# Reordering three early loads, one warm-up matmul less, and splitting a matmul chunk around the gathered rows' transposes

## The chip, the cores and the metric

The kernel runs on one core of a Trainium2 chip. The metric is the device time of one execution in microseconds (us); lower is better. The engines of the core are TensorE (PE, with its weight loads shown apart as PEld), VectorE (DVE), ScalarE (ACT), GpSimd (POOL) and SyncE (SP). Loads and stores are issued by SP, ACT or POOL and carried by the core's DMA engines.

## The reference

x is 2048 tokens of 640 features in bf16. It is normalized per token, and two branches on the normalized tokens xn are added to x:

```python
xn = _layernorm(x, axis=-1)
# branch A: linear attention, 32 heads of 20, phi(t) = where(t > 0, t + 1, exp(t)) + 1e-6
q, k, v = split(xn @ wqkv)
kv = einsum("bhsd,bhse->bhde", phi(k), v);  z = sum over s of phi(k)
a = (phi(q) @ kv) / (phi(q) @ z + 1e-6) @ wo
# branch B: one expert on the 8 tokens with the largest r = xn @ w_r
idx = argsort(-r)[:8]
y = (silu(xn[idx] @ w_gate) * (xn[idx] @ w_up)) @ w_down * sigmoid(r[idx])
b = xn + scatter_add(idx, y)
out = x + a + b
```

## The kernel before

The tokens are 16 tiles of 128. The order of the instructions on every engine is written out by hand; each engine and each queue works in the order of the program, and waits are semaphores between them.

*Start.* `ld_x(t0, t1, q)` (L114) loads tiles of x on queue q. SP issues tile 0, the first three fifths of the k weights (`wk[:, 0:3]`, L119), the router row `wrow` (L122), then tiles 2, 3, 4 and 5, the q weights `wq` and tiles 6 and 7. ACT's queue issues tile 1 and the last two fifths of the k weights (`wk[:, 3:5]`, L120). Meanwhile PE runs `N_WARM` matmuls on constants (L231) whose result nobody reads, and later `N_FILL` small ones (L368).

*Per tile.* `stats` (L238 to L241, DVE) makes mean and variance; `small` (L245 DVE, L246 POOL) makes the inverse deviation `rs` by a power on POOL; `center` subtracts the mean and `norm` (L266, DVE) scales by `rs`. `tr_mm` (L273, PE) transposes a tile by five 128x128 transposes into a PSUM bank, and `tr_ev` (L279 on ACT, L281 on DVE) copies it out. `k_mm(t, h)` (L302, PE) multiplies the tile with half h of the k weights in five steps over 128 features each: steps 0 to 2 need the first part of the weights, steps 3 and 4 the second. `k_act` (L313, L314, ACT) makes exp and relu, `k_stt` (L322, DVE) joins them to phi(k) in `pk`, and `g_mm` (L330, L332, PE) adds pk-transposed times xn to the sums over all tiles, which stay in PSUM. The first tiles are written out by hand: PE does the transposes of tile 0, turns the router row into a column of the k weights (L389), runs the two fills, then `k_mm(0, 0)`, the transposes of tile 1, `k_mm(0, 1)`, `k_mm(1, ...)`, the transposes of tile 2 and `g_mm(0, ...)`. DVE does `norm(0)`, `stats(2)`, `small(2)`, the two copies of tile 1's transposes, `center(2)`, `norm(2)`, `k_stt(0)`, `norm(1)` and so on. A loop over tiles 3 to 15 follows, with some chunks of q in it.

*Middle.* The sums leave PSUM (`gt`), the eight tokens are picked (L580 to L594, DVE), and POOL gathers their rows from memory into `xsel` by an indirect DMA (L597). In the meantime PE makes chunks of q: `q_next(bk)` takes the next chunk (128 features by 512 tokens) and calls `q_mm` (L345), five matmuls into PSUM bank bk; `q_fin` and `q_fin_d` turn it into phi(q) in `pqT`. `den_mm` (L675) makes denominators. `moe_xt(3)` transposes the gathered rows (L611) into bank 3, DVE copies them to `xsT` (L612), and `moe_gu_mm` (L628) multiplies them with the gate and up weights; `moe_silu` (L634 to L636, ACT) and the rest of the expert follow, with `kv_mm` (L714), `m_mm` (L733) and the stores `m_dma` (L747, SP) between them.

*End.* `out_mm` (L837) makes the output of the 16 tiles, ACT and DVE add the rest, and the tiles are stored.

Of the kernel before, what the change touches and what calls it, by code (L numbers as in the profile page):

```python
# [8 lines left out]
P = 128  # L9
# [5 lines left out]
KC = D // P  # L15
# [12 lines left out]
BF16 = mybir.dt.bfloat16  # L28
# [3 lines left out]
AF = mybir.ActivationFunctionType  # L32
ALU = mybir.AluOpType

N_WARM = 11
N_FILL = 2
PE_TR = 4
Q_ALL = [(m, b) for b in range(4) for m in range(KC)]
# [2 lines left out]
Q_TAIL = Q_ALL[Q_LOOP:]  # L41
# [7 lines left out]
def kernel(  # L49
# [16 lines left out]
    sp, act, dve, pool, pe = nc.sync, nc.scalar, nc.vector, nc.gpsimd, nc.tensor  # L66
# [9 lines left out]
    def sb(shape, dt, name):  # L76
        return big.tile(shape, dt, tag=name, name=name)
# [3 lines left out]
    def bank(i):  # L81
        return ps[:, i, :]

    def bankb(i):
        return ps[:, i, :].bitcast(BF16)
# [28 lines left out]
    def ld_x(t0, t1, q):  # L114
        q.dma_start(x_sb[:, t0:t1, :], x_v[:, t0:t1, :])

    ld_x(0, 1, sp)
    ld_x(1, 2, act)
    sp.dma_start(wk[:, 0:3, 0:D], wqkv_v[:, 0:3, D : 2 * D])  # L119
    act.dma_start(wk[:, 3:5, 0:D], wqkv_v[:, 3:5, D : 2 * D])  # L120
    wrow = sb([KC, P], BF16, "wrow")
    sp.dma_start(wrow[:], B_w_r.rearrange("(kc p) -> kc p", p=P))  # L122
    ld_x(2, 3, sp)
    ld_x(3, 4, sp)
    ld_x(4, 6, sp)
    sp.dma_start(wq[:], wqkv_v[:, :, 0:D])
# [2 lines left out]
    def ld_w(dst, src, kc0, kc1, eng=sp):  # L129
        eng.dma_start(dst[:, kc0:kc1, :], src.rearrange("(kc p) n -> p kc n", p=P)[:, kc0:kc1, :])  # L130
# [8 lines left out]
    def ld_wd(k0, eng):  # L139
        ld_w(wd, B_w_down, k0, k0 + 3, eng)  # L140
# [88 lines left out]
    one_x = nc.const_aps.tensor(1.0, [P, 512], BF16)  # L229
    for _ in range(N_WARM):  # L230
        pe.matmul(bank(7), lhsT=one_w, rhs=one_x, start=True, stop=True)  # L231
# [3 lines left out]
    def stats(t, half=None):  # L235
        if half in (None, 0):
            st[t] = tmp.tile([P, 2, nc.vector.BN_STATS_DIM], F32, tag="st", name=f"st{t}", bufs=3)
            dve.bn_stats(out=st[t][:, 0, :], in_=x_sb[:, t, 0:HW])  # L238
        if half in (None, 1):
            dve.bn_stats(out=st[t][:, 1, :], in_=x_sb[:, t, HW:D])  # L240
            dve.bn_aggr(out=mv[:, t, :], in_=st[t][:])  # L241

    def small(t):
        c = slice(t, t + 1)
        dve.tensor_scalar(out=veps[:, c], in0=mv[:, t, 1:2], scalar1=EPS_BF16, scalar2=None, op0=ALU.add)  # L245
        pool.tensor_tensor(out=rs[:, c], in0=veps[:, c], in1=pw[:, 0:1], op=ALU.pow)  # L246
# [23 lines left out]
    def tr_mm(t, b, k0=0, k1=KC):  # L270
        for kc in range(k0, k1):
            c = slice(kc * P, (kc + 1) * P)
            pe.transpose(bankb(b)[:, c], cbs[t][:, c] if t < 2 else xn[:, t, c], ident[:])  # L273

    def tr_ev(t, b, k0=0, k1=KC, eng=act):
        dst = (xcT if t < 2 else xnT)[:, k0:k1, t * P : (t + 1) * P]
        src = bankb(b)[:, k0 * P : k1 * P].rearrange("p (k f) -> p k f", k=k1 - k0)
        if eng is act:
            act.copy(dst, src)  # L279
        else:  # L280
            dve.tensor_copy(dst, src)  # L281
# [58 lines left out]

    eq = {}

    def q_mm(m, b, bk):
        for kc in range(KC):
            pe.matmul(bank(bk), lhsT=wq_m[:, kc, m, :], rhs=xnT[:, kc, b * TB : (b + 1) * TB],  # L345
                      start=(kc == 0), stop=(kc == KC - 1))

# [52 lines left out]
    tr_mm(1, 7, 0, 3)  # L400
    tr_mm(1, 6, 3, 5)
    stats(2)
    small(2)
    tr_ev(1, 7, 0, 3, dve)
    tr_ev(1, 6, 3, 5, dve)
    k_mm(0, 1)
    k_act(0, 1)
# [37 lines left out]
    for t in range(3, T):  # L445
# [23 lines left out]
        for i, (m, b) in enumerate(Q_SLOT.get(t, [])):  # L469
            q_mm(m, b, h0 ^ i)  # L470
            q_act(m, b, h0 ^ i)
            q_stt(m, b)
# [82 lines left out]
    qn = [0]  # L555

    def q_next(bk):
        m, b = Q_TAIL[qn[0]]
        qn[0] += 1
        q_mm(m, b, bk)  # L560
        return m, b, bk

    def q_fin(c):
        q_act(*c)
        q_stt(c[0], c[1])
# [43 lines left out]
    def moe_xt(bk):  # L609
        for kc in range(KC):  # L610
            pe.transpose(bankb(bk)[:, kc * 32 : (kc + 1) * 32], cs["xsel"][:, kc * P : (kc + 1) * P], ident[0:32, 0:32])  # L611
        dve.tensor_copy(xsT[:], bankb(bk)[:, 0 : KC * 32].rearrange("p (k c) -> p k c", k=KC))  # L612
# [11 lines left out]
    def moe_gu_mm(b0, b1):  # L624
        for a, (w, bk) in enumerate(((wg, b0), (wu, b1))):
            for kc in range(KC):
                for j in range(4):
                    pe.matmul(ps[32 * j : 32 * j + 32, bk, 0:FJ], lhsT=xsT[:, kc, :],  # L628
                              rhs=w[:, kc, j * FJ : (j + 1) * FJ], start=(kc == 0), stop=(kc == KC - 1),
                              tile_position=(0, 32 * j))  # L630
# [54 lines left out]
    def rep_out_pair():  # L685
        sp.dma_start(rdp[:].rearrange("h i b n -> i h (b n)"), rden[:, 0:2, :].rearrange("p b n -> p (b n)"))
# [68 lines left out]
    q2 = q_next(0)  # L755
# [5 lines left out]
    den_act(0, 2, 7)  # L761
    rep_out_pair()
    ld_wd(9, sp)
    moe_xt(3)
    q_fin(q1)
    q2 = q_next(2)
    moe_gu_mm(4, 0)
    q_fin_d(*q2)
    moe_silu(4, 0)
# [25 lines left out]
    q2 = q_next(5)  # L795
# [12 lines left out]
    q2 = q_next(0)  # L808
# [32 lines left out]
    for t in range(T):  # L841
        bk = OB[t % 3]
# [11 lines left out]
        for i in range(2 * KC):  # L854
            kc, b = (i % KC, i // KC) if last else (i // 2, i % 2)
# [47 lines left out]
```

## Time and profile before

| | before |
|---|---|
| median of 3 runs | 111.58 us (111.35 to 111.87) |
| the profiled execution's own time | 111.57 us |
| its span | 109.8 us |
| busy PE, DVE, ACT, POOL | 103.9, 86.8, 67.7, 23.2 us |
| granted TensorE clock | 1.00 throughout |

The profile is one execution. A row of the timeline gives the start, the length, engine, line, operation, output and inputs, the count, and in square brackets the idle time of the engine ahead of it with what ended it. A row of the windows gives a stretch, its length, the busy time of PE, PEld, DVE, ACT and POOL with instruction counts, the granted clock, the share of the DMA engines and GB/s. Ends of matmuls are modelled, so a row's length runs past the start of the next.

### The profile page before, as it was taken

Reading aid. Unit: us, or ns where it says so; the run is one execution under the profiler, and the core shown is the slowest. Engines: PE = TensorE matmul, PEld = TensorE weight load, DVE = VectorE, ACT = ScalarE, POOL = GpSimd, SP = SyncE. Lnnn points to the kernel's source line nnn. Section 1 sums busy time; section 2 is a strip of 40 time slices with the busy share of each in tenths; the row PEclk is TensorE's granted clock in tenths of the full one; section 3 lists DMA queues with packets and bytes.
Section 4 is the critical chain, followed back from the end, with each engine's and each line's share of the span. In section 5 each row is a group of like instructions: output and inputs, shape, how many; then the busy total and the mean of one; then the engine's idle time right before and its main releaser. Section 6 shows DMA issues by size and latency. Waiting matters only on the chain.

```text
span 109.8 us, 2392 instructions
## 1 busy us (share of the span) xinstructions
PE 103.9 (95%) x834; PEld 64.9 (59%) x834; DVE 86.8 (79%) x216; ACT 67.7 (62%) x164; POOL 23.2 (21%) x54
## 2 busy tenths in 40 slices
PE   6977999999999999999999999999999999999980
PEld 2355654666655665666658555567655677777750
DVE  0779988999999999963336896669995899997670
ACT  4258875866866685455551868888869555555510
POOL 3022322548867332220000022000081000000000
PEclk9999999999999999999999999999999999999999
DMA  2999804399997889999999998772354973899533
GB/s 86 342 370 353 145 17 123 72 290 296 240 310 183 179 220 225 258 291 303 350 382 365 359 153 160 195 218 97 104 147 81 294 252 62 290 340 356 194 119 119
DMA packets 29480, 24.55 MB, mean 223 GB/s; under 512 B 14700, under 2 KB 28060, under 8 KB 29468
## 3 DMA queue, kind: packets, MB, share of 16 engines
q1 hardware_dynamic: 27356, 22.16, 73.1%
q10 hardware_dynamic: 1936, 2.19, 5.8%
q0 software_dynamic: 176, 0.05, 0.6%
q8 instruction: 6, 0.10, 0.4%
q14 instruction: 6, 0.05, 0.1%
HBM read 15.00 MB, written 5.46 MB: 186 GB/s over the span
## 4 chain that ended last, share of the span: by engine, by line
PE 50%; DVE 31%; DMA 7%; issue 4%; POOL 2%; ACT 1%; SPq 1%; DVEq 0%; ACTq 0%
PE ps L837 19%; PE ps L345 7%; PE ps L302 7%; PE ps L330 7%; DVE pk L322 6%; DVE st L240 4%; DMA wrow<-in_B_w_r_dram 4%; DVE xn L266 4%; DVE st L238 4%; DMA xsel<-xd,idxi 3%; DVE cb L257 2%; DVE mv L241 2%; POOL rs L246 2%; PE ps L733 2%; PE ps L337 2%
## 5 line engine op out<-in xcount | busy, mean ns | idle before, releaser
L330 PE MATMUL ps<-xn,pk 128*128 128x512 bf16 x80 | 23.5, 381 | 0.2
L345 PE MATMUL ps<-xnT,wq 128*128 128x512 bf16 x100 | 23.7, 381 | 0.0
L837 PE MATMUL ps<-late,pqT 128*128 128x320 bf16 (+2 forms) x160 | 22.1, 299 | 0.0
L302 PE MATMUL ps<-wk,xnT 128*128 128x320 bf16 (+1 forms) x140 | 21.4, 299 | 0.0
L837 PEld LDWEIGHTS <-pqT 128*128 128x128 bf16 x160 | 15.5, 98 | 6.6 <-DVE pqT L357 0.5
L313 ACT ACTIVATE ek<-ps 128x320 bf16<-128x320 f32 x28 | 12.4, 441 | 9.4 <-PE ps L302 9.4
L322 DVE SCALAR_TENSOR_TENSOR pk<-ek,rk 128x640 bf16<-128x640 bf16 x16 | 13.1, 818 | 6.3 <-ACT rk L314 6.3
L302 PEld LDWEIGHTS <-xnT 128*128 128x128 bf16 x140 | 13.5, 97 | 7.5 <-ACT xnT L279 0.3
L246 POOL TENSOR_TENSOR rs<-veps,pw 128x1 f32<-128x1 bf16 x15 | 12.0, 799 | 27.2 <-DVE veps L245 27.2
L345 PEld LDWEIGHTS <-wq 128*128 128x128 bf16 x100 | 11.0, 119 | 8.8 <-issue 0.3
L352 ACT ACTIVATE eq<-ps 128x512 bf16<-128x512 f32 x18 | 10.7, 596 | 8.7 <-PE ps L345 7.8
L859 ACT CAST oall<-ps 128x640 bf16<-128x640 f32 x14 | 9.7, 692 | 9.0 <-PE ps L837 9.0
L357 DVE SCALAR_TENSOR_TENSOR pqT<-eq,rq 128x512 bf16<-128x512 bf16 x18 | 12.1, 687 | 3.5 <-ACT rq L353 3.5
L330 PEld LDWEIGHTS <-pk 128*128 128x128 bf16 x80 | 8.4, 117 | 6.7 <-DVE pk L322 1.6
L314 ACT ACTIVATE rk<-ps 128x320 bf16<-128x320 f32 x28 | 12.2, 437 | 0.0
L353 ACT ACTIVATE rq<-ps 128x512 bf16<-128x512 f32 x18 | 10.7, 593 | 0.0
L332 PE MATMUL ps<-xn,pk 128*128 128x129 bf16 x48 | 10.6, 220 | 0.0
L238 DVE BATCH_NORM_STATS2 st<-x_sb 128x6 f32<-128x320 bf16 x16 | 7.8, 485 | 2.8 <-DMA x_sb<-in_A_x_dram 2.8
L832 DVE TENSOR_TENSOR oall<-oall,x_sb 128x640 bf16<-128x640 bf16 x14 | 6.8, 487 | 2.0 <-ACT oall L859 1.9
L825 DVE TENSOR_TENSOR x_sb<-x_sb,xn 128x640 bf16<-128x640 bf16 x16 | 7.7, 484 | 0.2 <-DMA xn<-xd 0.2
L240 DVE BATCH_NORM_STATS2 st<-x_sb 128x6 f32<-128x320 bf16 x16 | 7.6, 476 | 0.0
L266 DVE TENSOR_SCALAR xn<-cb,rs 128x640 bf16<-128x640 bf16 x15 | 5.9, 399 | 1.0 <-POOL rs L246 0.9
(134 smaller groups left out, 112.1 us busy)
## 6 DMA issues: line engine op xcount, KB each, us to landing
xd<-xn SPq DMA_DIRECT2D x16, 160.0 KB
x_sb<-in_A_x_dram SPq DMA_DIRECT2D x6, 320.0 KB
wg<-in_B_w_gate_dram SPq DMA_DIRECT2D x5, 384.0 KB
xn<-xd SPq DMA_DIRECT2D x3, 640.0 KB
out_dram<-oall SPq DMA_DIRECT2D x11, 160.0 KB
wu<-in_B_w_up_dram SPq DMA_DIRECT2D x3, 384.0 KB
wd<-in_B_w_down_dram ACTq DMA_DIRECT2D x2, 480.0 KB
wd<-in_B_w_down_dram SPq DMA_DIRECT2D x2, 480.0 KB
```

What stands on the lines that cost most here:

```text
L238: dve.bn_stats(out=st[t][:, 0, :], in_=x_sb[:, t, 0:HW])
L240: dve.bn_stats(out=st[t][:, 1, :], in_=x_sb[:, t, HW:D])
L246: pool.tensor_tensor(out=rs[:, c], in0=veps[:, c], in1=pw[:, 0:1], op=ALU.pow)
L302: pe.matmul(ps[:, KB.get((t, h), h), 0:n], lhsT=(xcT if t < 2 else xnT)[:, kc, t * P : (t + 1) * P], rhs=wk[:, kc, h * HW : h * HW + n], s ...
L313: act.activation(e[:, s], ps[:, b, 0:HW], AF.Exp, scale=c)
L314: act.activation(r[:, s], ps[:, b, 0:HW], AF.Relu, scale=c)
L322: dve.scalar_tensor_tensor(out=pk[:, t, :], in0=e[:], scalar=1.0, in1=r[:], op0=ALU.min, op1=ALU.add)
L330: pe.matmul(bank(2 + m), lhsT=w, rhs=xn[:, t, 0:512], start=(t == 0), stop=(t == T - 1))
L345: pe.matmul(bank(bk), lhsT=wq_m[:, kc, m, :], rhs=xnT[:, kc, b * TB : (b + 1) * TB], start=(kc == 0), stop=(kc == KC - 1))
L352: act.activation(e[:], bank(bk), AF.Exp)
L357: dve.scalar_tensor_tensor(out=pqT[:, m, b * TB : (b + 1) * TB], in0=e[:], scalar=1.0, in1=r[:], op0=ALU.min, op1=ALU.add)
L837: pe.matmul(ps[:, bk + b, 0 : hi - lo], lhsT=pqT[:, kc, t * P : (t + 1) * P], rhs=m_sb[:, kc, lo:hi], start=(kc == 0), stop=(kc == KC - 1))
```

## The change

Four edits. The router row is issued on SP ahead of the first part of the k weights. Tile 2 of x is issued on ACT's queue, ahead of the second part of the k weights, instead of on SP behind the first. There are ten warm-up matmuls instead of eleven, and DVE does the first copy of tile 1's transposes ahead of `small(2)`. In the middle, the next chunk of q is no longer done whole behind the gathered rows' transposes: its first three matmuls are done ahead of them and the last two behind; `q_mm` takes the range of steps for it. Banks and the order on the other engines stay.

```diff
-N_WARM = 11
+N_WARM = 10
...
     ld_x(0, 1, sp)
     ld_x(1, 2, act)
+    wrow = sb([KC, P], BF16, "wrow")
+    sp.dma_start(wrow[:], B_w_r.rearrange("(kc p) -> kc p", p=P))
+    ld_x(2, 3, act)
     sp.dma_start(wk[:, 0:3, 0:D], wqkv_v[:, 0:3, D : 2 * D])
     act.dma_start(wk[:, 3:5, 0:D], wqkv_v[:, 3:5, D : 2 * D])
-    wrow = sb([KC, P], BF16, "wrow")
-    sp.dma_start(wrow[:], B_w_r.rearrange("(kc p) -> kc p", p=P))
-    ld_x(2, 3, sp)
     ld_x(3, 4, sp)
...
-    def q_mm(m, b, bk):
-        for kc in range(KC):
+    def q_mm(m, b, bk, k0=0, k1=KC):
+        for kc in range(k0, k1):
...
     stats(2)
+    tr_ev(1, 7, 0, 3, dve)
     small(2)
-    tr_ev(1, 7, 0, 3, dve)
     tr_ev(1, 6, 3, 5, dve)
...
     ld_wd(9, sp)
+    m, b = Q_TAIL[qn[0]]
+    qn[0] += 1
+    q_mm(m, b, 2, 0, 3)
     moe_xt(3)
     q_fin(q1)
-    q2 = q_next(2)
+    q_mm(m, b, 2, 3, KC)
+    q2 = (m, b, 2)
     moe_gu_mm(4, 0)
```

## The prediction

> **What bounds the kernel now.** I read the page's busy shares and its chain first, then the busy time by stage.
>
> ```profile
> span 109.8 us, 2392 instructions
> PE 103.9 (95%) x834; PEld 64.9 (59%) x834; DVE 86.8 (79%) x216; ACT 67.7 (62%) x164; POOL 23.2 (21%) x54
> PE 50%; DVE 31%; DMA 7%; issue 4%; POOL 2%; ACT 1%; SPq 1%; DVEq 0%; ACTq 0%
> ```
>
> Half of the chain is PE, a third DVE. The stages (length, then busy PE, PEld, DVE, ACT, POOL):
>
> ```profile
> 0.00:9.00 9.00, 6.86 (x34) 3.10 (x34) 5.08 (x17) 4.26 (x10) 1.67 (x12) 1.00 0.81 272
> 9.00:17.00 8.00, 7.77 (x57) 4.81 (x58) 7.28 (x20) 6.19 (x19) 2.16 (x3) 1.00 0.62 144
> 17.00:43.30 26.30, 26.20 (x162) 15.90 (x163) 25.24 (x68) 17.96 (x49) 14.19 (x36) 1.00 0.86 216
> 43.30:61.00 17.70, 17.70 (x139) 11.97 (x139) 10.16 (x27) 9.24 (x31) 1.23 (x2) 1.00 1.10 325
> 84.40:105.40 21.00, 21.00 (x171) 14.94 (x172) 18.28 (x35) 11.31 (x18) 0.00 (x0) 1.00 0.73 242
> ```
>
> From 9 us on PE is never idle for long; until 43.3 DVE is nearly as full (25.24 of 26.30). So a microsecond is won only where both wait: in the first 11 us, and at the gathered rows near 68.9. What is won there passes to the end, because the stages behind are dense and their inputs are made by the same two engines.
>
> The start, PE and its weight loads:
>
> ```profile
> 6.05 0.17 PE L389 MATMUL ps<-ident,wrow 5*128 5x5 bf16 x1 [0.58 <-DMA wrow<-in_B_w_r_dram]
> 6.39 0.97 PE L302 MATMUL ps<-wk,pqT 128*128 128x320 bf16 x5
> 6.92 0.10 PEld L302 LDWEIGHTS <-pqT 128*128 128x128 bf16 x1 [0.16 <-issue]
> 7.19 0.44 PE L273 MATMUL ps<-ident,cb 128*128 128x128 bf16 x5
> 9.02 0.85 PE L302 MATMUL ps<-wk,pqT 128*128 128x320 bf16 x5 [0.70 <-DVE pqT L281]
> 10.74 0.41 PE L330 MATMUL ps<-xn,pk 128*128 128x512 bf16 x1
> ```
>
> PE waits for the router row (6.05) and starts k_mm(0,0) at 6.39. Inside these five matmuls a weight load sits idle until 6.92, ahead of the fourth or fifth. The page names no releaser; the fourth is the first that needs the k weights' second part (wk2), and I take 6.92 for its landing. At 9.02 PE waits for DVE's copies of tile 1, at 10.74 for pk of tile 0.
>
> ```profile
> 6.40 0.38 DVE L266 TENSOR_SCALAR xn<-cb,rs 128x640 bf16<-128x640 bf16 x1
> 7.35 0.49 DVE L238 BATCH_NORM_STATS2 st<-x_sb 128x6 f32<-128x320 bf16 x1 [0.57 <-DMA x_sb<-in_A_x_dram]
> 8.61 0.56 DVE L281 COPY pqT<-ps 128x384 bf16<-128x384 bf16 x2
> 8.76 0.73 POOL L246 TENSOR_TENSOR rs<-veps,pw 128x1 f32<-128x1 bf16 x1 [1.84 <-DVE veps L245]
> 9.08 0.38 DVE L257 TENSOR_SCALAR cb<-x_sb,mv 128x640 bf16<-128x640 bf16 x1
> 9.56 0.39 DVE L266 TENSOR_SCALAR xn<-cb,rs 128x640 bf16<-128x640 bf16 x1
> 9.87 0.82 DVE L322 SCALAR_TENSOR_TENSOR pk<-ek,rk 128x640 bf16<-128x640 bf16 x1
> ```
>
> DVE is idle for 0.57 us until x of tile 2 lands, then runs on to k_stt(0) at 9.87, which g_mm(0) waits for. So x2's landing at 7.35 sets the start now. ACT is close behind:
>
> ```profile
> 4.64 0.29 ACT L384 ACTIVATE lnv<-mv,epsv 128x1 f32<-128x1 bf16 x1 [2.57 <-DVE mv L241]
> 7.45 0.53 ACT L313 ACTIVATE ek<-ps,rs 128x320 bf16<-128x320 f32 x1 [1.01 <-PE ps L302]
> 8.78 0.52 ACT L314 ACTIVATE rk<-ps,rs 128x320 bf16<-128x320 f32 x1
> ```
>
> It waits for k_mm(0,0) until 7.45 and ends its last operand of k_stt(0) at 8.78+0.52 = 9.30, which leaves 0.57 us to 9.87, 0.52 after a 0.05 hand-over.
>
> **The change part by part.** Three loads change places.
>
> ```profile
> 1.26 0.41 SPq L119 DMA_DIRECT2D wk<-in_A_wqkv_dram  x1
> 5.99 0.37 SPq L115 DMA_DIRECT2D x_sb<-in_A_x_dram  x1
> 6.00:6.90 0.90, 0.85 (x6) 0.59 (x7) 0.75 (x4) 0.34 (x2) 0.55 (x1) 1.00 1.03 378
> 6.90:7.40 0.50, 0.50 (x7) 0.40 (x6) 0.05 (x1) 0.00 (x0) 0.03 (x1) 1.00 1.05 359
> ```
>
> *Router row first on SP.* The first k weights (wk1) are issued one slot, about 0.45 us, later than 1.26. Their landing moves between nothing and 0.45; PE needs them near 6.39 and wk2 later, so this costs nothing unless wk1 comes after wk2. The row itself comes before the weights, and its PE wait (0.58) goes; late next is wk2 itself, so alone this is worth nothing.
>
> *x2 on ACT's queue ahead of wk2.* ACT issues one more load; the engine is idle for 2.57 us ahead of 4.64, which hides it. On SP the tiles 3 to 7 and wq move up one place; none is awaited before 9.87. But wk2 goes back. The engines move 359 to 378 GB/s here, full (share above 1), so one 160 KB tile costs about 0.45 us (163,840 bytes at 359 to 378 GB/s: 0.43 to 0.46). Now wk2 lands at 6.92 and x2 0.43 later, at 7.35. By 7.35 the two queues have carried x0, x1, wk1, wk2 and x2; the same bytes in another order are done at the same moment, so the last of them, now wk2, lands at about 7.35: 0.43 late. It can be better (0) if the ACT queue is served faster than SP's, and worse if tile 3 and tiles 4 and 5, now right behind wk1 on SP, go between: 0.45 for each tile. I take 0.43, from the row of the same bytes.
>
> Behind the wait stand PE's transposes of tile 1 and k_mm(0,1), and ACT for all of them: k_mm(0,0) ends 0.43 later, ACT's last operand at 9.73, and k_stt(0) can start at 9.78. On DVE x2 is there in time: norm(0) is issued at 6.40, and stats(2) follows at about 6.78, so its work ends some 7.95. Tile 1's transposes come 0.43 later, at 7.63+0.43 = 8.06, so the copies start at 8.11 instead of 8.61.
>
> *small(2) behind the first copy.* From the copy's start: 0.27 to the next instruction, 0.24 to POOL's power, 0.73 for it and 0.07 to norm(2), which is 9.42; norm(2) to k_stt(0) is 0.31 (9.56 to 9.87), so 9.73. ACT's 9.78 is later and decides: 0.09 won against 9.87. DVE and PE both go on from there. k_mm(1) starts before 9.02 and then waits at g_mm(0). Start: **-0.09**.
>
> *One warm-up matmul less.*
>
> ```profile
> 0.84 4.14 PE L231 MATMUL ps<-const-bfloat16-1.0 128*128 128x512 bf16 x11 [0.84 <-PEq L887]
> 3.78 0.15 PEld L231 LDWEIGHTS <-const-bfloat16-1.0 128*128 128x128 bf16 x1 [0.28 <-issue]
> 4.16 0.32 PEld L231 LDWEIGHTS <-const-bfloat16-1.0 128*128 128x128 bf16 x2 [0.23 <-issue]
> ```
>
> The eleven end at 4.98, just before the first transposes need PE, so nothing is gained. Loads come 0.38 apart until 4.16 and two within 0.32 afterwards: PE doubled its pace at about 4.16, ahead of the eleventh. Price zero, unless the pace doubles later (a rival). The Trainium skill, "TensorE: Matmul & The Clock Gate", Part 1, says that the gate opens after about 3.4 us of activity, with the moment varying by 0.5 us between runs; the 3.3 us from 0.84 to 4.16 agree, and 0.5 us later would be past the tenth matmul, which speaks against dropping one.
>
> *Three matmuls of the q chunk ahead of the gathered rows' transposes.*
>
> ```profile
> 67.87 0.74 PE L675 MATMUL ps<-pqT,zm 128*32 128x128 bf16 x40
> 68.92 0.27 PE L611 MATMUL ps<-ident,xsel 32*128 32x32 bf16 x5 [0.30 <-DMA xsel<-xd,idxi]
> 69.12 1.27 PE L345 MATMUL ps<-xnT,wq 128*128 128x512 bf16 x5
> 70.33 1.00 PE L628 MATMUL ps<-wg,xsT 128*32 128x384 bf16 x20
> 80.48 0.46 PE L675 MATMUL ps<-pqT,zm 128*32 128x128 bf16 x20
> 80.88 3.43 PE L345 MATMUL ps<-xnT,wq 128*128 128x512 bf16 x15
> 69.47 0.23 DVE L612 COPY xsT<-ps 128x160 bf16<-128x160 bf16 x1
> 71.38 0.49 ACT L634 ACTIVATE late<-ps 128x384 bf16<-128x384 f32 x1 [0.33 <-PE ps L628]
> 76.03 5.63 SPq L747 DMA_DIRECT2D late<-late  x6
> ```
>
> PE waits 0.30 us for xsel. A chunk of five takes 1.21 (69.12 to 70.33): five at 0.216 (fifteen take 3.43 and five 1.27, so ten take 2.16), and 0.13 for changing over. den_mm ends at 68.61 (67.87+0.74); in the later rows the next chunk starts 0.06 ahead of such an end (80.88 against 80.48+0.46), so the three could start at 68.55 and end with their changeover at 69.33; the transposes take 0.20 (68.92 to 69.12), the other two matmuls 0.56: gate and up matmuls at 70.09 instead of 70.33, 0.24 to 0.25 earlier. **-0.25**. Bounds: nothing if the new changeovers eat it, 0.38 if the second costs nothing. The xsT copy, now after about 69.6, ends by 69.9, still ahead of 70.09. ACT's wait ahead of 71.38 (0.33) and so the silu chain follow PE. Queued behind are SP's six stores from 76.03, released by ACT's copies: they move with PE.
>
> Sum: 111.57 (span 109.8 and 1.77 around it; the median is 111.58, so the profile is a typical run) - 0.09 - 0.25 = **111.23**.
>
> The Trainium skill, "DMA: Bandwidth & Descriptors", Queues, rings and completion order, says that each DMA engine takes turns between queues. By even turns ACT's 160+320 KB end together with SP's 480 KB of wk1, no further tile between: 0.43 late, the same 111.23. The trace disagrees in part: wk1 (480 KB) had let SP go on at 5.99 while wk2 (320 KB), issued beside it, came 0.93 later; so ACT's queue got less than its turn, and by that row rival 2 below has its chance.
>
> **The rivals.**
> 1. wk2 isn't late: ACT's queue is served in time. Then ACT is ready at 9.35, DVE decides: copies at 7.95, k_stt(0) at 7.95+1.31+0.31 = 9.57, 0.30 won: 111.57-0.30-0.25 = 111.02. For it: only the slowest DMA engine counts for a landing, and another order may treat it better. Against: the bytes.
> 2. wk2 much too late, the slower side: tiles 3 and 4 go between, 0.90 more, landing 8.25, 1.33 late. ACT ends at 10.63, k_stt(0) at 10.68, 0.81 lost: 111.57+0.81-0.25 = 112.13. Break-even is 0.77 late (0.52 of ACT's slack and 0.25 of the gather), a landing at 7.69. For it: ACT's queue was served behind SP's before.
> 3. The split does nothing: changeovers eat the gap. 111.57-0.09 = 111.48.
> 4. The clock opens late: 3.3 us (0.84 to 4.16) at half pace in the dense stretch after 9 us cost about 1.65: 112.9. For it: less early PE work. Against: 4.16 lies before the tenth matmul's end.
>
> **How the numbers follow.** Forecast case 0.45; rival 1 0.24; rival 2 0.13; rival 3 0.13; rival 4 0.05. A measurement tells about 0.5% (0.56 us) from no change: faster is below 111.01, slower above 112.14. Faster: over half of rival 1 (gather at up to 0.38 gives 110.89) 0.16, and the forecast case's lower side 0.15: 0.31. Slower: half of rival 2, rival 4: 0.12. Same: 0.57. The range 110.80 to 112.15 takes in rival 1 with the gather's upper bound and rival 2; the forecast case alone is 110.95 to 111.55.
>
> **What would show it.** DVE's wait ahead of stats(2) gone, the 0.58 ahead of the router row gone; the weight load inside k_mm(0,0) near 7.35 (6.9: rival 1; past 7.7: rival 2) and ACT's first ek 0.43 after 7.45; pk of tile 0 near 9.8; weight loads half as far apart from about 4.2. Counted from den_mm to gate and up: 2.21 us instead of 2.46, without PE's wait for xsel. Wrong if the stretch from pk of tile 0 to den_mm (58 us) changes length by more than 0.3, or if the end after 70.33 doesn't move with it.

## The result and the profile after

The change makes the kernel slower. Its median is 114.81 us (114.21 to 115.96, six runs) against 111.32 us (110.60 to 111.87, six runs) of the kernel before measured beside it: a ratio of 1.031, with a 95% interval from 1.024 to 1.038. The forecast was 111.23 us, and its range ended at 112.15. Ratios here leave out single disturbed runs; where the runs of one kernel split by their clock, the text gives both groups.

The profiled execution took 114.21 us. Lines behind the reordered loads have moved by one to four in the changed kernel. From its page:

```profile
span 112.5 us, 2380 instructions
PEclk9996699999999999999999999999999999999999
PE 52%; DVE 29%; DMA 9%; issue 4%; POOL 2%; SPq 1%; DVEq 0%
```

The span is 2.7 us longer. Two of its 40 slices (near 8.4 to 14 us) have a TensorE clock of 0.6; before, all were 0.9 or more. In the chain the DMA's share rose from 7% to 9%. The chain of the last finished work starts like this (start, length, what):

```profile
1.65 6.96 DMA wk<-in_A_wqkv_dram
8.65 0.84 PE ps L302 x5
9.85 3.63 PE ps L302 x15
```

It names a load: the first part of the k weights (wk1), issued by SP at 1.65, is done 6.96 later, at 8.61. The timeline of the changed kernel shows what each wait of the start became:

```profile
3.93 1.88 SPq L115 DMA_DIRECT2D x_sb<-in_A_x_dram  x1
5.77 0.18 PE L389 MATMUL ps<-ident,wrow 5*128 5x5 bf16 x1
6.79 0.49 DVE L238 BATCH_NORM_STATS2 st<-x_sb 128x6 f32<-128x320 bf16 x1
8.65 0.84 PE L302 MATMUL ps<-wk,pqT 128*128 128x320 bf16 x5 [2.27 <-DMA wk<-in_A_wqkv_dram]
9.59 0.53 ACT L313 ACTIVATE ek<-ps,rs 128x320 bf16<-128x320 f32 x1 [3.09 <-PE ps L302]
12.21 0.82 DVE L322 SCALAR_TENSOR_TENSOR pk<-ek,rk 128x640 bf16<-128x640 bf16 x1 [0.97 <-ACT rk L314]
13.60 0.38 PE L330 MATMUL ps<-xn,pk 128*128 128x512 bf16 x1
70.81 0.74 PE L675 MATMUL ps<-pqT,zm 128*32 128x128 bf16 x40
71.48 0.84 PE L345 MATMUL ps<-xnT,wq 128*128 128x512 bf16 x2
72.26 0.28 PE L611 MATMUL ps<-ident,xsel 32*128 32x32 bf16 x5
72.47 0.63 PE L345 MATMUL ps<-xnT,wq 128*128 128x512 bf16 x2
73.03 1.00 PE L628 MATMUL ps<-wg,xsT 128*32 128x384 bf16 x20
87.01 1.25 PE L841 MATMUL ps<-late,pqT 128*128 128x320 bf16 x8
```

The last row, `out_mm`, was this before:

```profile
84.36 2.88 PE L837 MATMUL ps<-late,pqT 128*128 128x320 bf16 x20
```

PE's wait for the router row is gone (5.77 has no bracket) and DVE's for x of tile 2 as well (6.79 instead of 7.35). But k_mm(0,0) starts at 8.65 instead of 6.39, behind a wait of 2.27 us; k_stt(0) comes at 12.21 instead of 9.87, g_mm(0) at 13.60 instead of 10.74 (+2.86). From there to den_mm it is 57.21 us, 57.13 before, so den_mm is 2.94 late; from den_mm to the gate and up matmuls it is 2.22 us, 2.46 before, and PE's wait for xsel is gone; out_mm starts at 87.01 instead of 84.36 (+2.65). So the loss arises ahead of 13.6 us, and the gathered rows give 0.24 back.

Two things went wrong in the start. The first is in the DMA engines, as the windows show (last columns: granted clock, DMA share, GB/s; the five early loads are tiles 0 to 2 of x, wk1 and wk2). Before:

```profile
0.00:7.35 7.35, 5.89 (x27) 2.59 (x28) 3.50 (x11) 2.71 (x6) 1.43 (x11) 1.00 0.76 254
3.50:5.50 2.00, 1.93 (x11) 0.63 (x8) 1.93 (x6) 0.59 (x3) 0.00 (x0) 1.00 1.04 367
```

After:

```profile
0.00:7.35 7.35, 5.55 (x18) 2.09 (x19) 3.97 (x13) 2.62 (x6) 1.43 (x11) 1.00 0.72 221
7.35:8.61 1.26, 0.00 (x0) 0.00 (x0) 0.53 (x2) 0.00 (x0) 0.00 (x0) 1.00 0.96 317
3.50:5.50 2.00, 2.00 (x9) 0.68 (x7) 1.92 (x6) 0.50 (x2) 0.00 (x0) 1.00 0.87 256
9.00:13.00 4.00, 4.00 (x22) 2.48 (x21) 2.08 (x7) 2.41 (x6) 0.55 (x1) 0.57 1.29 263
```

From 3.5 to 5.5 us the engines move 256 GB/s instead of 367. By 7.35 us, when all five early loads had landed before, 221 x 7.35 = 1624 KB have moved instead of 254 x 7.35 = 1867 KB: 243 KB short. The five loads landed at 8.61, another 317 x 1.26 = 399 KB later. So 243 of these 399 KB are lost rate, and the other 156 KB are loads that nobody waits for yet and that went ahead.

The rate is an average, and the weights are late in a few parts only. Each of these loads leaves sixteen completion marks in the trace, as many as the profile counts DMA engines, and it has landed with the last of them. Of wk1's marks twelve had come by 6.48 us; the last four came at 7.36, 8.29, 8.53 and 8.61. Of wk2's, twelve had come by 6.80 and the last four came from 8.00 to 8.35. Before the change all of wk1's came from 4.99 to 5.98, and of wk2's fifteen by 6.37 and the last at 6.88.

The second is the clock, the third column from the end: 0.57 from 9 to 13 us. PE stood still for 2.27 us and went on at 8.65. At 9.55 its clock was halved, until 12.96 by the trace's record of the granted clock, and the fifteen matmuls behind took 3.63 us in the chain.

### The profile page after: what moved, and what is told of

It reads as the page before. It is cut to its first block, busy times and chain, and to the rows that moved or that the text cites. A ratio compares the mean times of both kernels' runs of the same rounds, so it can differ in the third digit from the quotient of the medians.

```text
span 112.5 us, 2380 instructions
## 1 busy us (share of the span) xinstructions
PE 105.2 (94%) x822; PEld 65.7 (58%) x833; DVE 87.0 (77%) x216; ACT 67.7 (60%) x164; POOL 23.0 (20%) x54
## 4 chain that ended last, share of the span: by engine, by line
PE 52%; DVE 29%; DMA 9%; issue 4%; POOL 2%; SPq 1%; DVEq 0%
PE ps L841 18%; PE ps L302 10%; PE ps L345 7%; DMA wk<-in_A_wqkv_dram 6%; PE ps L330 6%; DVE pk L322 5%; DVE st L240 4%; DVE st L238 4%; DMA xsel<-xd,idxi 3%; DVE xn L266 3%; DVE mv L241 2%; POOL rs L246 2%; DVE cb L257 2%; PE ps L733 2%; PE ps L337 2%
## 5 line engine op out<-in xcount | busy, mean ns | idle before, releaser
L330 PE MATMUL ps<-xn,pk 128*128 128x512 bf16 x74 | 22.1, 381 | 0.3
L302 PE MATMUL ps<-wk,pqT 128*128 128x320 bf16 (+1 forms) x20 | 4.7, 407 | 2.3 <-DMA wk<-in_A_wqkv_dram 2.3
```

Of the source, the lines that this page charges most:

```text
L302: pe.matmul(ps[:, KB.get((t, h), h), 0:n], lhsT=(xcT if t < 2 else xnT)[:, kc, t * P : (t + 1) * P], rhs=wk[:, kc, h * HW : h * HW + n], s ...
L330: pe.matmul(bank(2 + m), lhsT=w, rhs=xn[:, t, 0:512], start=(t == 0), stop=(t == T - 1))
```

## The experiments

The diffs are against the kernel named. Where a ratio stands, it is to the kernel before, measured on the same chip beside it. e6, e7, e8 and e10 have two runs each.

**Each edit alone.** e1: the kernel before with the router row ahead of wk1, and nothing else.

```diff
+    wrow = sb([KC, P], BF16, "wrow")
+    sp.dma_start(wrow[:], B_w_r.rearrange("(kc p) -> kc p", p=P))
     sp.dma_start(wk[:, 0:3, 0:D], ...)
     act.dma_start(wk[:, 3:5, 0:D], ...)
-    wrow = ...; sp.dma_start(wrow[:], ...)
```

> Only the router row's move: it goes ahead of the first k weights on SP; the rest as before. Theory R (the row, a load of five short lines ahead of the weights, holds up SP's queue): the first k weights land near 8.6 us instead of 5.98, k_mm(0,0) starts near 8.6, the clock is halved for about 3.4 us after it, time 113.5 to 115. Theory X (tile 2 on ACT's queue takes the engines' turns from the first k weights): k_mm(0,0) starts at 6.2 to 6.9 and the time is 111.0 to 111.8.

Measured: 111.40 against 111.10 us, ratio 1.0015 (0.998 to 1.005). k_mm(0,0) starts at 6.58. One more run, of 182.13 us at a mean clock of 0.565, stands alone. The row alone costs nothing that can be measured, so it alone is not the cause.

e2: the kernel before with tile 2 on ACT's queue ahead of the second part of the k weights (wk2), and nothing else.

```diff
+    ld_x(2, 3, act)
     act.dma_start(wk[:, 3:5, 0:D], ...)
...
-    ld_x(2, 3, sp)
```

> Only tile 2's move to ACT's queue; the row stays behind the first k weights. Theory X: the first k weights land after 7.5 us, k_mm(0,0) starts after 7.5, time 113 to 115. Theory R: the first k weights near 6, the second part near 7.35, k_mm(0,0) ends some 0.4 us later than before, time 111.0 to 111.8. A third theory, that both together are needed (SP's weights issued later and ACT's queue fuller), gives both this and the row alone under 112.

Measured: 112.02 against 111.10 us, ratio 1.006 (1.002 to 1.009). Its timeline and windows:

```profile
7.58 0.43 PE L302 MATMUL ps<-wk,pqT 128*128 128x320 bf16 x2 [0.72 <-DMA wk<-in_A_wqkv_dram]
9.98 0.82 DVE L322 SCALAR_TENSOR_TENSOR pk<-ek,rk 128x640 bf16<-128x640 bf16 x1 [0.35 <-ACT rk L314]
68.02 0.74 PE L675 MATMUL ps<-pqT,zm 128*32 128x128 bf16 x40
70.74 1.00 PE L628 MATMUL ps<-wg,xsT 128*32 128x384 bf16 x20
0.00:7.50 7.50, 5.99 (x22) 2.26 (x23) 3.88 (x13) 2.62 (x6) 1.43 (x11) 1.00 0.77 249
3.50:5.50 2.00, 2.00 (x9) 0.59 (x7) 1.68 (x5) 0.49 (x2) 0.00 (x0) 1.00 1.06 387
```

Here the prediction's step for tile 2 holds nearly to the letter: wk2 is the last of the five loads and lands at about 7.53 (predicted 7.35), when 249 x 7.50 = 1868 KB have moved, as many as the 1867 KB of before. PE's step is 7.58 - 6.92 = 0.66 later, so by the prediction's formula ACT would be ready at 9.30 + 0.66 = 9.96; DVE starts k_stt(0) at 9.98, waiting for ACT, 0.11 later than before. That passes on to den_mm, 0.15 late. In this profiled run the rest doesn't come from the start: the stretch from den_mm to gate and up, which the edit doesn't touch, is 2.72 us instead of 2.46. Neither edit alone makes three per cent in the median; but one of the ten runs of e2 took 115.90 us at a mean clock of 0.970. It was not profiled, but a loss of the full size seems possible with tile 2's move alone.

The near hit on wk2 is partly luck: fifteen of its sixteen marks had come by 6.60, and one came at 7.53.

e3: the kernel before with the q chunk split around the gathered rows' transposes, and nothing else.

```diff
+    m, b = Q_TAIL[qn[0]]; qn[0] += 1
+    q_mm(m, b, 2, 0, 3)
     moe_xt(3)
     q_fin(q1)
-    q2 = q_next(2)
+    q_mm(m, b, 2, 3, KC); q2 = (m, b, 2)
```

> Only the split of the q chunk around the gathered rows' transposes. The stretch from the first den matmul to the gate and up matmuls takes 2.21 us instead of 2.46 and the end moves with it: 0.2 to 0.25 us below the kernel before. The rival that the split returns nothing: equal within 0.05 us, with SP's stores or DVE late in the place of PE.

Measured: 111.27 against 111.10 us, ratio 1.001 (0.998 to 1.004). In the trace the stretch is as short as predicted:

```profile
67.63 0.74 PE L675 MATMUL ps<-pqT,zm 128*32 128x128 bf16 x40
69.86 1.00 PE L628 MATMUL ps<-wg,xsT 128*32 128x384 bf16 x20
```

2.23 us instead of 2.46, but a gain of 0.23 us, 0.2%, can't be told from no change in the time itself: the interval reaches from -0.2% to +0.4%.

**The clock.** e4: the changed kernel with 18 fill matmuls instead of 2, which PE does while it would wait for the weights.

```diff
-N_FILL = 2
+N_FILL = 18
```

> The changed kernel with 18 fill matmuls instead of 2 ahead of k_mm(0,0), to keep PE busy until the weights land. If the halved clock is a consequence of PE's idle 2.3 us, the clock stays at 1.00 (mean over 0.99), k_mm(0,0) still starts near 8.65, and the time falls by 0.7 to 1.7 us from 114.3 to about 113. If the clock has another cause, it is halved again for 3.4 us and the time stays at 114 to 115.5.

Measured: 112.95 against 111.10 us, ratio 1.014 (1.009 to 1.020).

```profile
9.12 0.84 PE L302 MATMUL ps<-wk,pqT 128*128 128x320 bf16 x5 [0.62 <-DMA wk<-in_A_wqkv_dram]
69.97 0.74 PE L675 MATMUL ps<-pqT,zm 128*32 128x128 bf16 x40
3.50:5.50 2.00, 2.00 (x9) 0.63 (x7) 1.87 (x6) 0.50 (x2) 0.00 (x0) 1.00 0.84 246
9.50:13.50 4.00, 3.49 (x33) 2.69 (x32) 2.86 (x9) 3.45 (x9) 0.55 (x1) 1.00 1.21 255
```

k_mm(0,0) comes 0.47 us later even than in the changed kernel, yet the clock stays at 1.00. From k_mm(0,0) to den_mm it is 69.97 - 9.12 = 60.85 us, against 70.81 - 8.65 = 62.16 in the changed kernel: the halved clock costs some 1.31 us there (an estimate, since the two starts are 0.47 apart). The late load is a loss of its own: the DMA rate is as low (246 GB/s) with PE busy.

e12: the changed kernel with the eleventh warm-up matmul back.

```diff
-N_WARM = 10
+N_WARM = 11
```

> The changed kernel with eleven warm-up matmuls again. If PE's idle time before the late weights halves the clock: no help, clock near 0.97 to 0.985 and 114 to 115.5. If the missing warm-up does: clock 1.00 and 112.5 to 113.2, as with the 18 fills.

Measured: 114.33 against 111.14 us, ratio 1.028 (1.021 to 1.035).

```profile
8.46 1.20 PE L302 MATMUL ps<-wk,pqT 128*128 128x320 bf16 x5 [2.15 <-DMA wk<-in_A_wqkv_dram]
9.50:13.00 3.50, 3.50 (x21) 2.33 (x20) 1.74 (x6) 2.33 (x6) 0.55 (x1) 0.61 1.17 230
```

The clock is halved all the same, in all four runs (mean clock 0.970 to 0.985), so it was not the missing warm-up. With e4, PE's wait for the weights is the cause that is left.

**Why the weights are late.** e5: the changed kernel with tile 2 behind wk2 on ACT's queue.

```diff
-    ld_x(2, 3, act)
     sp.dma_start(wk[:, 0:3, 0:D], ...)
     act.dma_start(wk[:, 3:5, 0:D], ...)
+    ld_x(2, 3, act)
```

> The changed kernel, with the second part of the k weights ahead of tile 2 on ACT's queue again; the row stays first on SP and tile 2 on ACT. Theory T (in the changed kernel both parts of the k weights begin at the same moment, and these two streams out of one matrix slow all DMA engines: 246 to 256 GB/s from 3.5 to 5.5 us where the others have 367 to 387): here the second part begins in the pause behind the row, so over 350 GB/s from 3.5 to 5.5 us, k_mm(0,0) at 6.3 to 6.9, clock 1.00, time 110.6 to 111.3. Theory C (the row first and tile 2 on ACT are enough together, in whatever order): under 300 GB/s, k_mm(0,0) after 8, time 114.

Measured: 111.75 against 110.92 us, ratio 1.004 (1.001 to 1.008).

```profile
7.90 0.84 PE L302 MATMUL ps<-wk,pqT 128*128 128x320 bf16 x5 [1.45 <-DMA wk<-in_A_wqkv_dram]
3.50:5.50 2.00, 2.00 (x9) 0.65 (x7) 1.89 (x6) 0.50 (x2) 0.00 (x0) 1.00 0.99 350
```

With the same loads on the same queues, one exchange on ACT's queue brings the rate back to 350 GB/s and most of the time too. The expectation of k_mm(0,0) at 6.3 to 6.9 was missed all the same: it still starts 1.5 us later than before (fifteen of wk1's marks had come by 7.07, the last at 7.86). Three of twelve runs, at 113.32 to 113.83 us, have a mean clock of 0.981 to 0.985.

e6: the changed kernel with tiles 6 and 7 of x loaded later, behind the store of the first tile's xn (`xn_store(0)`, L293 in the SP rows). In the changed kernel SP issues that load at 3.93, in the one before at 5.99, so it could have taken the bandwidth.

```diff
-    ld_x(6, 8, sp)
...
     xn_store(0)
+    ld_x(6, 8, sp)
```

> The changed kernel, with the load of tiles 6 and 7 issued after the first store of xn; in the changed kernel it is issued at 3.93 us and SP is held in it for 1.88 us, before it was issued at 5.99. Theory S (this early load overfills SP's queue and slows the engines): over 350 GB/s from 3.5 to 5.5 us, k_mm(0,0) before 7.2, time 110.8 to 112. Theory T: no change, about 250 GB/s, k_mm(0,0) after 8, time 114 to 115.5.

Measured: 113.40 against 110.92 us, ratio 1.022 (1.017 to 1.028); 315 GB/s from 3.5 to 5.5 us, k_mm(0,0) at 8.34 behind a wait of 1.57 us. The early load is at most a part.

e7: the changed kernel with the k weights cut 2:3 instead of 3:2.

```diff
-    sp.dma_start(wk[:, 0:3, 0:D], ...)
-    act.dma_start(wk[:, 3:5, 0:D], ...)
+    sp.dma_start(wk[:, 0:2, 0:D], ...)
+    act.dma_start(wk[:, 2:5, 0:D], ...)
```

> The changed kernel, with the k weights cut 2 to 3 between SP and ACT instead of 3 to 2; so the two streams are 0.98 MB apart in memory instead of 1.47 MB. If two streams out of one matrix at once are enough (theory T): about 250 GB/s from 3.5 to 5.5 us and 114 us again. If it is the distance of the two streams (theory A): over 350 GB/s and the time falls below 112.5.

Measured: 114.69 against 110.92 us, ratio 1.034 (1.028 to 1.040); 241 GB/s; PE waits 1.71 us for the first part and 0.47 for the second. Another distance between the two streams in memory doesn't bring the rate back.

e8: the kernel before, with tile 2 on SP ahead of wk1 and tile 3 on ACT ahead of wk2; the row stays behind wk1.

```diff
+    ld_x(2, 3, sp)
+    ld_x(3, 4, act)
     sp.dma_start(wk[:, 0:3, 0:D], ...)
     act.dma_start(wk[:, 3:5, 0:D], ...)
...
-    ld_x(2, 3, sp)
-    ld_x(3, 4, sp)
```

> The kernel before, with one tile of x ahead of the k weights on each queue (tile 2 on SP, tile 3 on ACT) and the row behind them, so that both parts of the k weights begin at the same moment without the row ahead. Theory T: under 300 GB/s in the 2 us after the two begin (about 4.2 us), k_mm(0,0) ends after 9, time 113 to 115. If the row ahead is needed for the slow transfer: over 350 GB/s, the weights land about 0.9 us later than before, time 111.5 to 112.3.

Measured: 115.62 and 113.04 us against 110.92. Both weight parts are late again (landings 8.28 and 8.79; of wk1's marks fifteen had come by 6.79), and the row's too; the rate falls to 278 GB/s, now from 5.5 to 7.5 us, after the two parts have begun. So a row ahead of them isn't needed for the loss.

e9: the changed kernel with wk2 on SP right behind wk1, so that the two parts run one after the other.

```diff
-    act.dma_start(wk[:, 3:5, 0:D], ...)
+    sp.dma_start(wk[:, 3:5, 0:D], ...)
```

> The changed kernel, with the second part of the k weights issued on SP right behind the first; row first and tile 2 on ACT as changed. Theory T (two streams out of the k weights that begin together slow the engines): one stream, so over 350 GB/s from 3.5 to 5.5 us, all weights there by 7.0, clock 1.00, time 110.6 to 111.4. If the row ahead and tile 2 on ACT were slow in themselves: under 300 GB/s and 113 to 115.

Measured: a median of 113.17 against 111.14 us, but in two groups: five runs at 111.45 to 111.91 us with a mean clock of 0.996 to 1.000, seven at 113.12 to 113.48 us with 0.980 to 0.985. The ratio 1.005 (1.000 to 1.010) speaks for the first group and one run of the second. The profiled run is of the second:

```profile
7.57 1.56 PE L302 MATMUL ps<-wk,pqT 128*128 128x320 bf16 x5 [1.73 <-DMA wk<-in_A_wqkv_dram]
3.50:5.50 2.00, 1.96 (x12) 0.72 (x10) 1.93 (x6) 0.66 (x3) 0.00 (x0) 1.00 0.85 245
7.50:9.50 2.00, 1.78 (x11) 1.15 (x11) 0.22 (x2) 0.28 (x1) 0.00 (x0) 0.59 1.07 383
```

This is the same program with and without the halved clock: 113.36 - 111.57 = 1.79 us between the medians of the groups. That may be more than the clock's price, if the weights also landed later in the second group; only one run of it was profiled. wk1 is late here without wk2 beside it, so the two parts running side by side aren't needed for a low rate either: while SP's queue stands behind the row, ACT's has run out of work.

e10: the changed kernel with tile 3 on ACT's queue too, ahead of wk2.

```diff
     ld_x(2, 3, act)
+    ld_x(3, 4, act)
...
-    ld_x(3, 4, sp)
```

> The changed kernel, with tile 3 as well as tile 2 ahead of the second part of the k weights on ACT's queue, so that the second part begins some 0.4 us or more after the first, as it did before the change. If it is the same beginning that counts: over 340 GB/s from 3.5 to 5.5 us, the first weights by 6.5, the second by about 7.8, time 111.5 to 112.8 with the clock at 1.00. If any overlap of the two behind the row is slow: under 300 GB/s, 113.5 to 116.

Measured: 114.68 against 111.14 us, ratio 1.029 (1.020 to 1.038). wk1 comes at 6.45, but wk2 at 8.7, and PE waits 1.70 us inside k_mm(0,0).

e13: the changed kernel with the router row on ACT's queue, between tiles 1 and 2, so that nothing stands ahead of wk1 on SP but tile 0.

```diff
-    sp.dma_start(wrow[:], B_w_r...)
+    act.dma_start(wrow[:], B_w_r...)
```

> The changed kernel with the router row issued on ACT's queue, between x of tiles 1 and 2, instead of on SP; nothing else differs, and all bytes ahead of k_mm(0,0) are the same. Theory T (the loss comes from the k weights' two parts starting side by side, behind the pause that the row leaves on SP's queue): wk1 now starts at once, as before; it lands at 6.0 to 6.5 us, the engines move at least 340 GB/s in 3.5 to 5.5 us, only wk2 is late (7.5 to 8.0, behind x2 and the pause), the clock stays at 1.0, and the time is that of x2's move alone less the gather's 0.24: 0.998 to 1.010 of before. Rival U (an early row together with x2's move loses whichever queue the row is on, for instance because it is early): rate below 300 GB/s, wk1 after 7.5 us, clock below 0.99, ratio 1.02 or more.

Measured: 113.44 against 111.08 us, ratio 1.022 (1.018 to 1.027); three runs at clock 1.000 (112.51 to 113.15 us) and three at 0.983 to 0.985 (113.74 to 113.99 us). The profiled one, of 112.69 us, is of the first three:

```profile
6.28 0.58 PE L302 MATMUL ps<-wk,pqT 128*128 128x320 bf16 x3
8.78 0.43 PE L302 MATMUL ps<-wk,pqT 128*128 128x320 bf16 x2 [1.92 <-DMA wk<-in_A_wqkv_dram]
12.08 0.41 PE L330 MATMUL ps<-xn,pk 128*128 128x512 bf16 x1 [0.26 <-DVE pk L322]
0.00:8.73 8.73, 5.12 (x21) 2.01 (x22) 4.50 (x14) 2.62 (x6) 1.43 (x11) 1.00 0.78 249
3.50:5.50 2.00, 1.11 (x8) 0.33 (x6) 1.67 (x5) 0.48 (x2) 0.00 (x0) 1.00 1.06 355
```

Half of the expectation held: wk1 in time, 355 GB/s. The time did not, because wk2 paid instead: it landed at about 8.73 instead of 7.5 to 8.0. By then 249 x 8.73 = 2174 KB had moved, 307 KB more than the 1867 KB with which the five loads were done in the kernel before: tiles 3 to 5, behind wk1 on SP, landed at 6.32 and 8.52, ahead of wk2. By the packet records ACT's queue, which now has the row, moves nothing from 3.5 to 4.5 us, and SP's moves 370 KB.

**A better version.** e11: the kernel before with the two edits that nothing speaks against, the split and the first copy of tile 1's transposes ahead of `small(2)`.

```diff
+    tr_ev(1, 7, 0, 3, dve)
     small(2)
-    tr_ev(1, 7, 0, 3, dve)
...
     (and the split, as in e3)
```

> The kernel before with the two edits that touch no load and no warm-up: the split of the q chunk and the first copy ahead of small(2). From the first den matmul to gate and up 2.23 us instead of 2.46; the start as before within its scatter. Time 0.15 to 0.3 us below before (ratio 0.997 to 0.999); if the split's gain were lost later, the ratio is 1.000 or more while that stretch is still 2.23.

Measured: 111.16 against 111.14 us, ratio 0.999 (0.996 to 1.003). den_mm to gate and up is 2.23 us here too (67.48 to 69.71). What the copy's move does can't be told: k_stt(0) starts at 9.45 instead of 9.87, but stats(2) starts at 7.06 instead of 7.35, as tile 2 landed earlier in this execution. No version beats the kernel before by what can be measured.

## Why the prediction was wrong

**The step that failed** is "the same bytes in another order are done at the same moment", with "this costs nothing unless wk1 comes after wk2" ahead of it. It was applied to two edits apart, and apart both hold (e1, e2, but for one run of e2). Together they don't: the five early loads were done not at 7.35 but at 8.61, after 2023 KB (235 GB/s on average up to there, as a window from 0 to 8.61 has it) instead of 1867. Both halves of the sentence were wrong, the bytes (156 KB of other loads went ahead) and the rate (256 instead of 367 GB/s for 2 us). wk1 then came after wk2 (8.61; wk2 at 8.35), the condition that the prediction named and gave no price.

Two things in the profile before spoke against the rule on bytes. The five loads are 1280 KiB or 1311 KB, but 1867 KB had moved when the last of them landed at 7.35: later loads went ahead then already. And a landing is that of the slowest of sixteen parts, which differs between executions. e3 and e11 have the same early loads as the kernel before; there wk2 landed at 6.19 and 6.44 instead of 6.88, and tile 2 at 6.92 and 7.03 instead of 7.33. The forecast took one execution's 6.92 and 7.35 as fixed.

**Rival 2** had nearly the right landing of wk2: it put it at 8.25, and it landed at 8.35. Its way there is borne out in part. By 8.61 us 2023 KB had moved, 712 more than the five loads, so parts of later loads did go ahead; but tile 3 as a whole landed at 9.08, behind wk2, and wk1, on which the rival put no delay, was later still. So the number is partly luck. e13 shows its formula at work. There only wk2 is late, by 8.78 - 6.92 = 1.86 us; ACT's last operand of k_stt(0) is then ready at 9.30 + 1.86 = 11.16 and k_stt(0) can start at 11.21, 1.34 later than 9.87; g_mm(0) is 12.08 - 10.74 = 1.34 later. With 0.25 from the gathered rows that gives 111.57 + 1.34 - 0.25 = 112.66 us; the profiled run took 112.69. The chance of 0.13 was too small: it was outweighed by the rule on bytes. The row quoted for it, wk2 landing 0.93 us behind the larger wk1 before, is weaker than it looked, though: in e3 it was 0.12 (6.19 and 6.07).

**Rival 4**, the clock, had the right size and the wrong trigger. It priced the halved clock at 1.65 us; e4 says 1.31, and the medians of two groups lie 1.79 apart in e9 and 113.86 - 112.69 = 1.17 in e13. But it looked at a late opening only, and that did come about in the changed kernel's profiled run:

```profile
0.83 4.43 PE L231 MATMUL ps<-const-bfloat16-1.0 128*128 128x512 bf16 x10 [0.83 <-PEq L891]
5.12 0.72 PE L273 MATMUL ps<-ident,cb 128*128 128x128 bf16 x5
```

The warm-up never doubles its pace, and tile 0's transposes take 0.72 us instead of 0.45. The trace records the clock's opening at 6.13 us, against 4.10 before. (Ahead of an opening there is no record, and the views print 1.00 there; the pace of the matmuls is half.) That cost nothing, since PE then waited for wk1. Nor can it be put down to the missing matmul: the recorded openings lie from 3.83 to 5.48 us with eleven warm-up matmuls and from 3.55 to 6.84 with ten, so the 4.16 on which the price of zero rested was one draw. (The weight loads ahead of it come 0.43 us apart, at 2.07, 2.50 and 2.93 for instance; the prediction's 0.38 is the last step alone.) PE's idle time ahead of a late weight load is what closed the clock again (e4, e12); the mean clock is 0.968 to 0.985 in all six runs of the changed kernel. Rivals 2 and 4 were taken as alternatives; the late load brings the clock with it, so their prices add.

**The sum, redone.** In the profiled run: k_mm(0,0) 8.65 - 6.39 = 2.26 later; the halved clock 1.31 (e4); from k_mm(0,0) to den_mm otherwise 60.85 us (e4) instead of 67.87 - 6.39 = 61.48, -0.63 (probably because PE meets fewer waits behind a start that late; that is not shown); the gathered rows -0.24. That is +2.70, and 111.57 + 2.70 = 114.27 for a run of 114.21. The median of 114.81 lies higher, since three of the six runs (115.27 to 115.96) have a mean clock of 0.968 to 0.970, lower than the 0.982 of the profiled run. In e7's profiled run a mean of 0.969 is 6.83 us at half clock, twice the 3.41 here.

**What was right.** The split: -0.25 predicted, -0.24 in the changed kernel and -0.23 alone. DVE's wait for tile 2 and PE's for the row went. One warm-up matmul less costs nothing by itself (e12 is as slow with it). What is won or lost in the start passes to the end: den_mm is 2.94 late, and out_mm 2.65, behind a gain of 0.24. That 0.25 us can be seen in a trace and not in the time was said of the measurement, and e3 and e11 are such cases.

**What stays open.** Why a few parts of the loads come so late, and why the rate falls. The packet records show a queue that moves almost nothing for 0.5 to 1 us behind the row: 5 to 23 KB on SP's queue from 3.0 to 3.5 us in the nine runs that have the row early on it (16 KB in the changed kernel), nothing on ACT's from 3.5 to 4.5 in e13. But ACT's queue, without the row, falls to 32 and 20 KB in the two halves of that microsecond in the changed kernel, so the row is not the only thing that goes with such a pause. Single packets take up to 1.3 us (0.69 before) where most take 0.055; what holds them up is not recorded. Neither the row (e8) nor the two parts side by side (e9) is needed, the distance in memory isn't it (e7), tiles 6 and 7 are a part at most (e6). I expected that both parts starting at one moment is what it takes; e9 and e10 (311 GB/s) speak against so simple a rule.

## What to carry to other kernels

Moving one load to another queue changes every stream beside it. Two moves that are harmless apart, or nearly so, cost over 2 us together here, so forecast the landing of each load that an engine waits for, with a price for each of them being last, and give the loads behind it on the other queue a chance to go ahead. A late load at the start is paid twice if PE stands idle while it waits: some dummy matmuls (e4) save the clock, though not the load. A landing time read from one execution is one draw of the slowest of sixteen parts, so take it from several. In a stage where PE is full, a shortened chain of 0.24 us arrives in full, but is below what a comparison of times can tell.

## What the runs showed of the hardware that was not expected

*The clock changes in steps of 3.41 us.* By the trace's record it opens at 6.13 us in the changed kernel, is halved from 9.55 to 12.96 and full behind that. In all six profiled runs in which it was halved in the start (the changed kernel, e7, e8, e9, e10, e12) it closed 3.41 us after it had opened, and stayed so for 3.41 us, or for 6.83 in e7 and e8. PE had been busy for 1.15 to 1.64 of the 3.41 us ahead of the closing. Where the clock stayed, it was busy for 1.60 us (e13), 1.84 (e6), 1.96 (e5) and 2.79 (e4) of the step that has most of the wait. So in these runs a step with PE busy for less than about half of it closes the clock; the line isn't sharp, since e9 closed at 1.64 and e13 did not at 1.60.

The length of the wait alone tells less. By PE's longest wait for a load in the profiled run (the other runs were not profiled), and in how many runs the mean clock was 0.985 or lower: 2.76 us (e8) 1 of 2; 2.27 (the changed kernel) 6 of 6; 2.15 (e12) 4 of 4; 1.92 (e13) 3 of 6; 1.73 (e9) 7 of 12; 1.71 (e7) 2 of 2; 1.70 (e10) 2 of 2; 1.57 (e6) 1 of 2; 1.45 (e5) 3 of 12; 0.72 (e2) 1 of 10; 0.62 with fills (e4) none of 4. It also happens in e1's run of 182.13 us, in 1 of 12 runs of e3 and of e11, and in 3 of the 80 runs of the kernel before beside the experiments. The Trainium skill, "TensorE: Matmul & The Clock Gate", Why this matters for your kernels, advises against idle gaps of over about 3 us between bursts of matmuls; gaps of 1.5 to 2.3 us went with it here. Part 1 of that page has a free-running activity window of about 3.4 us. The trace agrees, with its steps of 3.41 us, and where the wait falls in such a step would explain that the same program gets the lowered clock in some runs only.

*While both queues had packets, they shared the engines about evenly; a pause upsets the balance.* In e13 ACT's queue had carried tiles 1 and 2 and wk2, 640 KiB or 655 KB beside the row, when wk2 landed, of 2174 KB in all, so 30%. But from 5.0 to 7.5 us, when both queues had packets, the records give 407 KB on ACT's and 397 KB on SP's (168 and 196 KB from 4.0 to 5.0 in the kernel before). The difference arises while ACT's queue pauses, and near the end, when few packets of wk2 are left. The Trainium skill, "DMA: Bandwidth & Descriptors", Queues, rings and completion order, has each engine take turns between queues packet by packet; the trace agrees for these stretches. The prediction read wk2's late landing before the change as ACT's queue getting less than its turn; of wk2's sixteen parts fifteen were there by 6.37, and one was late.
